# Weight sums, short convolution, input split and order of products in an FFN beside a long convolution

## The chip, the cores and the metric

The kernel runs on one core of a Trainium2 chip. Its time is the device time of one execution in microseconds (us). Three executions of the kernel before took 1178.04, 1177.70 and 1166.35 us, a median of 1177.7. The engines are named as in the profile: PE (TensorE's matmuls), PEld (its weight loads), DVE (VectorE), ACT (ScalarE), POOL (GpSimd), SP (SyncE, which here only issues transfers).

## The reference

Two branches read the normalized input and are added to it. All is float32, S = 2048 tokens, D = 576 channels, 4608 hidden units.

```python
x = A_q
xn = _layernorm(x)
# A: short causal convolution of k (4 taps), times v, long causal convolution by FFT, times xn
k_shift = sum over t of k_pad[:, t:t + S, :] * shift_k[:, 3 - t]
kv = k_shift * v
y = irfft(rfft(kv, 2 * S) * rfft(ssm_k, 2 * S))[:S] + kv * ssm_D
# B: FFN
h = maximum(xn @ w1, 0)
out = x + xn * y + h @ w2
```

## The kernel before

**FFN.** Tokens lie in 16 tiles t of 128; a tile is two half-tiles u of 64 rows. Four blocks b of 512 tokens are worked in two halves: blocks 0 and 1, then 2 and 3. Within a half, 18 steps g each take 256 hidden units, so there are 36 steps, called quads; g = 0 is done by plain products (classical), 1 to 35 by quad (L497). Every float32 factor is split in a high part of 12 bits and a rest, and a product of two is made of three matmuls (product, L455: two chunks of three, 128x512). One quad multiplies 2 x 2 blocks (two token blocks, two groups of 128 hidden units, with w1's rows in halves) by Winograd's scheme with seven products, named "00", "01", "s2", "s3", "11", "s1", "s4" after the operand of x, and adds the last 64 of the 576 rows by rest (L463, two matmuls). The scheme needs four sums of weights (sums, L407, on POOL: four adds of 128x256) and their splits wb and wc; wa, wd, wr and w2 are split from the weights as loaded (split_w, L399: a copy on ACT, a subtraction on POOL). Two banks of PSUM hold the products. Between products ACT copies a bank: y gets -x (L514, L538), u2 and p5 are kept in SBUF (L531, L558); DVE adds them in the bank (L559, L570); hidden (L467) applies Relu on ACT to hh and takes the rest ll on DVE.

Between the products stand eight units: unit(n) calls mm2 (L594), 12 matmuls of 128x288 for one tile of the quad before, summed in one of two buffers pso. The result is added to acc by DVE (L614). In units 1 and 5 of a quad (SEEDED) ACT instead copies acc into pso before the matmuls (L592) and out again (L611). The order of all FFN matmuls is fixed (done["pe"] in matmuls, L446).

**Convolution.** The generator conv (L650) yields costs; tick (after each product, rest and unit) lets it run when enough FFN cost has passed (rate, W_FB to W_FO, PAUSE). Its five stages are

- fb: normalize tokens 1024 to 2047, transpose them by DRAM, write the seven operands for the second half to DRAM (later_operands);
- fk: transform ssm_k: load kt, split by stack (L630, half of the partitions on ACT, half on DVE), two matmuls, store zk;
- fx: for each of 16 tiles t the short convolution: tap (L723, DVE: multiply and add), gate (times v), split for both half-tiles by stack (two ACT copies and two DVE subtractions of 64x576), four transforms (first, L636), stores of zx;
- fm: for 36 chunks of 512 columns: second transform of k and x, product of the spectra, and the way back. Every second chunk is "stacked": its high and low parts are stacked in the partitions by four transfers of POOL (turn, L846), so that the way back is two matmuls (back_stacked, L863) instead of three (back); its low sums go to zl;
- fo: for 32 half-tiles: load z, add zl to it by an accumulating transfer of POOL (add_z, L926), split (L946, L947), two matmuls (L994, L995), add of y, gate with x, add to acc or to the finished first half.

The scheduler of the language orders the instructions of an engine by its own clock; here() and at_turn(g) only keep side work behind the last acc or Relu. Weights are loaded from POOL's queue, everything else mostly from SP's queue, which issues in order and waits in order.

The last unit's results leave by SP and ACT.

## Time and profile before

| | |
|---|---|
| three executions | 1178.04, 1177.70, 1166.35 us |
| the profiled execution | 1173.84 us, of it 1171.8 between the first and the last instruction (the span) |
| mean granted clock of TensorE | 0.969 |
| matmuls | 6028, PE busy 1062.8 us |
| data moved by DMA | 194.94 MB |

Every row of times below is from that one execution. A group row gives the line of the kernel, the engine, the operation, what it writes and reads with sizes, how often, the busy time and the mean in ns. A row of waits gives the engine that stood, for whom, how long in total, how many times and the longest time. A row of a single line gives least, median and greatest duration in ns, and its first and last start. In the timeline the first two numbers are start and length in us. A busy PE isn't one at its peak, since ends of matmuls are modelled; the distance between two starts is exact. In the rows, psf is the PSUM of the convolution, psh the banks of the quads, pso the sums of the units, r a loaded weight, ohi and olo the high part and the rest of z.

### The profile page before, as it was taken

Reading aid. Unit: us, or ns where it says so; the run is one execution under the profiler, and the core shown is the slowest. Engines: PE = TensorE matmul, PEld = TensorE weight load, DVE = VectorE, ACT = ScalarE, POOL = GpSimd, SP = SyncE. Lnnn points to the kernel's source line nnn. Section 1 sums busy time; section 2 is a strip of 40 time slices with the busy share of each in tenths; the row PEclk is TensorE's granted clock in tenths of the full one; section 3 lists DMA queues with packets and bytes.
Section 4 is the critical chain, followed back from the end, with each engine's and each line's share of the span. In section 5 each row is a group of like instructions: output and inputs, shape, how many; then the busy total and the mean of one; then the engine's idle time right before and its main releaser. Section 6 shows DMA issues by size and latency. Waiting matters only on the chain. (4 is left out here: it accounts for less than half of the span.)

```text
span 1171.8 us, 17791 instructions
## 1 busy us (share of the span) xinstructions
PE 1062.8 (91%) x6028; PEld 932.2 (80%) x6028; DVE 839.0 (72%) x1154; ACT 730.9 (62%) x1358; POOL 629.6 (54%) x741
## 2 busy tenths in 40 slices
PE   7879899899997888899889999999999999789988
PEld 3758799789886777788789887888888887577977
DVE  5765653577666999988753777777777763889885
ACT  4524453688883455555444888889888974545751
POOL 4345465655544555656454555546566655565850
PEclk8989999899999999999889999999999999889999
DMA  6266459644448445448752566766677647865844
GB/s 166 59 156 156 155 194 179 110 144 150 143 147 209 129 149 168 152 131 297 259 162 83 167 184 170 197 167 182 198 201 199 188 130 214 197 178 134 237 111 102
DMA packets 139062, 194.94 MB, mean 166 GB/s; under 512 B 69757, under 2 KB 72447, under 8 KB 137180
## 3 DMA queue, kind: packets, MB, share of 16 engines
q1 hardware_dynamic: 111932, 126.71, 38.6%
q0 software_dynamic: 26720, 66.21, 22.0%
q10 hardware_dynamic: 320, 0.88, 0.3%
q8 instruction: 48, 0.79, 0.3%
q14 instruction: 42, 0.34, 0.1%
HBM read 129.27 MB, written 50.33 MB: 153 GB/s over the span
## 5 line engine op out<-in xcount | busy, mean ns | idle before, releaser
L451 PE MATMUL pso<-w,hh 128*128 128x288 f32 x2304 | 482.0, 299 | 18.4 <-DVE acc L614 18.4
L451 PEld LDWEIGHTS pso<-w,hh 128*128 128x128 f32 x2304 | 390.6, 191 | 49.0 <-DVE acc L614 27.8
L451 PE MATMUL pso<-w,ll 128*128 128x288 f32 x1152 | 343.3, 298 | 0.0
L614 DVE TENSOR_TENSOR acc<-pso,acc 128x576 f32<-128x576 f32 x220 | 165.6, 753 | 91.9 <-PE pso L451 90.3
L451 PEld LDWEIGHTS pso<-w,ll 128*128 128x128 f32 x1152 | 220.0, 191 | 1.5
L471 ACT ACTIVATE hh<-psh 128x512 fp32r<-128x512 f32 x140 | 83.4, 596 | 118.9 <-PE psh L451 64.7
L403 POOL TENSOR_TENSOR wc<-sums,wc 128x512 fp32r<-128x512 f32 x35 | 47.8, 1366 | 156.0 <-ACT wc L402 156.0
L451 PE MATMUL psh<-xs,wb 128*128 128x512 f32 x420 | 116.1, 408 | 14.6 <-ACT u L531 14.4
L403 POOL TENSOR_TENSOR w<-r,w 128x576 fp32r<-128x576 f32 x72 | 109.9, 1527 | 16.4 <-ACT w L402 16.4
L472 DVE SCALAR_TENSOR_TENSOR ll<-psh,hh 128x512 fp32r<-128x512 f32 x140 | 95.8, 684 | 31.3 <-ACT hh L471 30.8
L451 PE MATMUL psh<-x,wa 128*128 128x512 f32 x420 | 110.6, 399 | 6.6 <-ACT psh L514 3.2
L451 PEld LDWEIGHTS psh<-xs,wb 128*128 128x128 f32 x420 | 77.5, 194 | 32.0 <-ACT u L531 19.2
L451 PEld LDWEIGHTS psh<-x,wa 128*128 128x128 f32 x420 | 76.4, 190 | 23.5 <-ACT psh L514 5.9
L414 POOL TENSOR_TENSOR sums<-r 128x256 f32<-128x256 f32 x70 | 57.8, 861 | 60.8 <-DMA r<-in_w 55.7
L451 PE MATMUL psh<-hl,wr 128*128 128x512 f32 x280 | 89.6, 398 | 0.7 <-ACT p L558 0.7
L611 ACT ACTIVATE acc<-pso 128x576 f32<-128x576 f32 x68 | 44.1, 648 | 54.5 <-PE pso L451 53.8
L634 DVE TENSOR_TENSOR ks<-kt,ks 64x288 fp32r<-64x288 f32 x64 | 56.2, 878 | 26.5 <-ACT ks L633 25.2
L414 POOL TENSOR_TENSOR sums<-sums,r 128x256 f32<-128x256 f32 x70 | 69.1, 987 | 0.8
L403 POOL TENSOR_TENSOR wa<-r,wa 128x512 fp32r<-128x512 f32 x36 | 51.6, 1432 | 31.6 <-ACT wa L402 31.5
L846 POOL DMA_DIRECT2D st<-yl x72 | 36.0, 514 | 59.9 <-issue 49.2
L451 PE MATMUL psh<-x,wc 128*128 128x512 f32 x210 | 57.3, 409 | 7.9 <-ACT psh L538 7.9
L451 PE MATMUL psh<-xs,wc 128*128 128x512 f32 x210 | 56.1, 402 | 7.8 <-DVE ll L472 7.7
(163 smaller groups left out, 2133.1 us busy)
## 6 DMA issues: line engine op xcount, KB each, us to landing
r<-in_w POOLq DMA_DIRECT2D x70, 288.0 KB, 4.6
r<-in_w POOLq DMA_DIRECT2D x35, 512.0 KB, 4.9
zk<-zk SPq DMA_DIRECT2D x32, 288.0 KB, 2.5
zx<-zx SPq DMA_DIRECT2D x32, 288.0 KB, 2.9
ztk<-zk SPq DMA_DIRECT2D x36, 256.0 KB, 3.0
ztx<-zx SPq DMA_DIRECT2D x36, 256.0 KB, 3.2
k<-k SPq DMA_DIRECT2D x72, 128.0 KB, 2.9
zo<-zy SPq DMA_DIRECT2D x32, 288.0 KB, 4.6
```

What stands on the lines that cost most here:

```text
L403: nc.gpsimd.tensor_tensor(w[:, 1, :n], src, w[:, 0, :n], OP.subtract)
L414: nc.gpsimd.tensor_tensor(t[:, to], a, b, OP.add)
L451: last = nc.tensor.matmul(ps, a, m, start=start and n == 0, stop=n == len(seq) - 1, skip_group_check=True)
L471: done["act"] = nc.scalar.activation(hh, ps, AF.Relu)
L472: nc.vector.scalar_tensor_tensor(ll, ps, 0.0, hh, op0=OP.max, op1=OP.subtract)
L611: done["act"] = nc.scalar.activation(two(acc[t]), ps[:, :, :NH], AF.Copy)
L614: done["acc"] = nc.vector.tensor_tensor(two(acc[t]), ps[:, :, :NH], two(acc[t]), OP.add)
L634: nc.vector.tensor_tensor(dst[other], src[own], dst[own], OP.subtract)
L846: nc.gpsimd.dma_start(st[q * A2:(q + 1) * A2, i % GR, :], yl[i * A2:(i + 1) * A2, :])
```

## The change

- The sums of weights go from POOL to DVE, behind the last add of acc. In the second half (g > 18) wb and wc are not made again: the first half stores them to DRAM (parts_n), the second half loads them.
- The products of a quad stand in the order "00", "01", "s2", "s1", "s3", "s4", "11". What u2 and p5 are added to is written to SBUF, and Relu reads it there. Splits for the next quad are placed anew, and units 4, 5 and 6 follow one another. Units work block 0 before block 1; the first quad has its four units at the beginning.
- Which units are seeded by ACT depends on the stage: six of eight in fb and fx, none in fk and fm, four in fo.
- fx: only the first tap is written by DVE; the other three products are added to it by accumulating transfers from POOL. The sum is split in one ACT copy and one DVE subtraction of 128x576, stored to DRAM and loaded back as the two stacks. Each half of zx is stored by itself.
- fm: all chunks use three matmuls on the way back; turn, back_stacked and zl are gone. More buffers for loads.
- fo: add_z is gone.
- later_operands loads rows earlier and works in smaller pieces; the planner's weights, pauses and warm-up counts are set anew; in the start the splits of the first weights stand earlier, and sums(1) later.

The diff, cut to its core (of quad only the new text stands here; removed functions are in the kernel above):

```diff
-W_FK, W_FX, W_FM, W_FO = 1.4, 4.2, 2.24, 2.4
+W_FK, W_FX, W_FM, W_FO = 2.4, 2.9, 3.5, 2.6
-PAUSES = 19
-SHARE = 0.985
+PAUSES = 18
+SHARE = 0.975
-N_FB, W_FB = 32, 2.0
+N_FB, W_FB = 36, 2.5
-WARM_TILE = (0, 10, 0, 4)
+WARM_TILE = (0, 6, 0, 0)
...
         t = sums_w[g] = wp.tile([P, 4, 2, P], F32, tag="sums", name=f"sums{g}")
         w00, w01 = r1[:, 0:2, :P], r1[:, 0:2, P:]
         w10, w11 = r1[:, 2:4, :P], r1[:, 2:4, P:]
-        for to, a, b in ((3, w00, w01), (0, t[:, 3], w11), (2, t[:, 0], w10), (1, w11, w01)):
-            nc.gpsimd.tensor_tensor(t[:, to], a, b, OP.add)
+        with at_sums(g):
+            for to, a, b in ((3, w00, w01), (0, t[:, 3], w11), (2, t[:, 0], w10), (1, w11, w01)):
+                nc.vector.tensor_tensor(t[:, to], a, b, OP.add)
+
+    def at_sums(g):
+
+        return tc.issue_after(done["acc"].ins) if g > 1 else nullcontext()
 
     def split_a(g):
         wa[g] = split_w(g, "wa", raw1[g][:, 0:4, :P], (4, P))
 
+    def kept(g):
+        return g > NQ
+
+    def split_sums(g, kind, pair):
+
+        if kept(g):
+            w = wp.tile([P, 2, 4, P], F32R, tag=kind, name=f"{kind}{g}")
+            nc.sync.dma_start(w.bitcast(F32), parts_n[kind][g % NQ])
+        else:
+            w = split_w(g, kind, sums_w[g][:, pair].rearrange("p s c f -> p (s c) f"), (4, P))
+            if g < NQ:
+                nc.sync.dma_start(parts_n[kind][g], w.bitcast(F32))
+        return w
+
     def split_b(g):
-        src = (sums_w[g][:, 0:2].rearrange("p s c f -> p (s c) f") if g else
-               raw1[g][:, 0:2, P:])
-        wb[g] = split_w(g, "wb", src, (4, P))
+        if g:
+            wb[g] = split_sums(g, "wb", slice(0, 2))
+        else:
+            wb[g] = split_w(g, "wb", raw1[g][:, 0:2, P:], (4, P))
 
     def split_c(g):
-        wc[g] = split_w(g, "wc", sums_w[g][:, 2:4].rearrange("p s c f -> p (s c) f"), (4, P))
+        wc[g] = split_sums(g, "wc", slice(2, 4))
 
     def split_d(g):
...
     def hidden(g, b, f, ps):
-        k = dict(bufs=2 if b else 4)
-        hh = hp.tile([P, 512], F32R, tag=f"hh{b}", name=f"hh{g}_{b}_{f}", **k)
-        ll = hp.tile([P, 512], F32R, tag=f"ll{b}", name=f"ll{g}_{b}_{f}", **k)
+        k = dict(bufs=2 - (b or f))
+        hh = hp.tile([P, 512], F32R, tag=f"hh{b}{f}", name=f"hh{g}_{b}_{f}", **k)
+        ll = hp.tile([P, 512], F32R, tag=f"ll{b}{f}", name=f"ll{g}_{b}_{f}", **k)
...
         b0, b1 = (0, 1) if g < NQ else (2, 3)
         more = g + 1 < QUADS
+        x = bank(g, 0, "1")
+        y = bank(g, 1, "2")
         if units and units[0] is not None:
             open_unit(*units[0], 0)
+        product(x, wa[g], 0, "00", start=True)
+        nc.scalar.activation(y, x, AF.Copy, scale=-1.0)
+        later("00")
+        unit(0)
         split_w2(g, 0)
         if more:
             load_w2(g + 1, 0)
+        product(x, wa[g], 2, "01")
+        rest(x, g, b0, 0)
+        hidden(g, 0, 0, x)
+        later("01")
         unit(1)
+        product(y, wb[g], 0, "s2")
         u2 = hp.tile([P, 512], F32, tag="u2", name=f"u2_{g}", bufs=1)
+        nc.scalar.activation(u2, y, AF.Copy)
+        later("s2")
+        x = bank(g, 0, "5")
+        product(x, wc[g], 2, "s1", start=True)
+        p5 = hp.tile([P, 512], F32, tag="p5", name=f"p5_{g}", bufs=1)
+        nc.scalar.activation(p5, x, AF.Copy)
+        later("s1")
+        unit(2)
         split_w2(g, 1)
         if more:
             load_w2(g + 1, 1)
+            if not kept(g + 1):
+                sums(g + 1)
+        product(y, wb[g], 2, "s3")
+        later("s3")
+        unit(3)
+        if more:
+            split_a(g + 1)
+        rest(x, g, b0, 1)
+        later(2)
+        product(x, wd[g], 0, "s4")
+        later("s4")
+        nc.vector.tensor_tensor(u2, x, u2, OP.add)
+        x = bank(g, 0, "4")
+        nc.scalar.activation(x, y, AF.Copy, scale=-1.0)
+        hidden(g, 0, 1, u2)
+        unit(4)
+        if more:
             split_b(g + 1)
         unit(5)
         if more:
             split_d(g + 1)
+        unit(6)
+        rest(y, g, b1, 1)
+        nc.vector.tensor_tensor(p5, y, p5, OP.add)
+        product(x, wc[g], 0, "11")
+        later("11")
+        unit(7)
+        hidden(g, 1, 1, p5)
+        rest(x, g, b1, 0)
+        later(3)
+        hidden(g, 1, 0, x)
+        if more:
             split_r(g + 1)
+            split_c(g + 1)
             if g + 2 < QUADS:
                 load_w1(g + 2)
...
+    stage = {"seeded": ()}
 
     def open_unit(g, b, i, n):
 
         t = token(g, b, i)
         ps = open_ps[g, t] = ps_o.tile([P, 2, 512], F32, tag="o", name=f"pso{g}_{t}")
-        if n in SEEDED and 0 < g < QUADS - 1:
+        if n in stage["seeded"] and 0 < g < QUADS - 1:
             seeded.add(t)
             nc.scalar.activation(ps[:, :, :NH], two(acc[t]), AF.Copy)
...
+    def stacks(pool, src, t):
+
+
+        both = pool.tile([P, 2, D], F32R, tag="both", name=f"both{t}", bufs=1)
+        with here():
+            nc.scalar.activation(both[:, 0], src, AF.Copy)
+            nc.vector.tensor_tensor(both[:, 1], src, both[:, 0], OP.subtract)
+        nc.sync.dma_start(xs_n[t % 2].rearrange("u p k d -> (u p) k d"), both.bitcast(F32))
+        out = []
+        for u in range(U):
+            stk = pool.tile([P, D], F32R, tag="stk", name=f"xs{t}_{u}", bufs=3)
+            for k in range(2):
+                nc.sync.dma_start(stk[halves(k)[0]].bitcast(F32), xs_n[t % 2][u, :, k])
+            out.append(stk)
+        return out
...
+            stage["seeded"] = (0, 1, 3, 4, 5, 7)
             yield from later_operands(fp)
...
                     else:
-                        e = fp.tile([P, D], F32, tag="e", name=f"e{t}_{n}", bufs=1)
+                        e = fp.tile([P, D], F32, tag="e", name=f"e{t}_{n}", bufs=3)
                         nc.vector.tensor_tensor(e, win[t - n], sk[:, n, :], OP.mult)
-                        nc.vector.tensor_tensor(sums[t], sums[t], e, OP.add)
+                        nc.gpsimd.dma_start(sums[t], e, accum_op=OP.add)
...
-            def split(t, u):
+            def split(t):
                 if t < T:
-                    stks[t, u] = fp.tile([P, D], F32R, tag="stk", name=f"xs{t}_{u}", bufs=4)
-                    with here():
-                        stack(stks[t, u], sums[t], u)
+                    stks[t, 0], stks[t, 1] = stacks(fp, sums[t], t)
...
-            gate(0)
-            for u in range(U):
-                split(0, u)
-            yield -PAUSE / 8
             for n in range(KS):
                 tap(1, n)
                 yield -PAUSE / 8
+            gate(0)
+            split(0)
+            yield -PAUSE
             for t in range(T):
                 if t + 2 < T:
                     load(t + 2)
 
-                side = (((gate, t + 1),), ((split, t + 1, 0),),
-                        ((split, t + 1, 1),), ((tap, t + 2, 0),),
-                        ((tap, t + 2, 1),), (),
-                        ((tap, t + 2, 2),), ((tap, t + 2, 3),))
+                side = (((tap, t + 2, 0),), ((tap, t + 2, 1),),
+                        ((gate, t + 1),), ((split, t + 1),),
+                        ((tap, t + 2, 2),), ((tap, t + 2, 3),), (), ())
                 for u in range(U):
-                    z = fp.tile([P, D], F32, tag="z", name=f"zx_{t}_{u}")
                     for h in range(2):
                         cols = slice(h * NH, (h + 1) * NH)
-                        first(mats[t], stks[t, u][:, cols], z[:, cols], u)
+                        z = fp.tile([P, NH], F32, tag="z", name=f"zx_{t}_{u}_{h}", bufs=3)
+                        first(mats[t], stks[t, u][:, cols], z, u)
+                        nc.sync.dma_start(at_t(zx, T * u + t)[:, :, cols], z)
                         for part in range(2):
                             for what, *args in side[4 * u + 2 * h + part]:
                                 what(*args)
                             yield W_FX / 2
-                    nc.sync.dma_start(at_t(zx, T * u + t), z)
...
             def parted(n):
...
-                if stacked(n):
-                    yh = fp.tile([P, GR, CW], F32R, tag="st", name=f"st{n}")
-                    for r in range(GR):
-                        nc.scalar.activation(yh[:, r, :], y, AF.Copy)
-                    nc.vector.tensor_tensor(yl, y, yh[:, 0, :], OP.subtract)
-                else:
-                    yh = fp.tile([P, CW], F32R, tag="yh", name=f"yh{n}")
-                    nc.scalar.activation(yh, y, AF.Copy)
-                    nc.vector.tensor_tensor(yl, y, yh, OP.subtract)
+                yh = fp.tile([P, CW], F32R, tag="yh", name=f"yh{n}")
+                nc.scalar.activation(yh, y, AF.Copy)
+                nc.vector.tensor_tensor(yl, y, yh, OP.subtract)
...
-    quad(1, [None, None, *((0, 1, i) for i in range(BT))])
+    quad(1, [*((0, 1, i) for i in range(BT))])
     for g in range(2, QUADS):
-        quad(g, [(g - 1, b, i) for b in (1, 0) for i in range(BT)])
-    for b in (1, 0):
+        quad(g, [(g - 1, b, i) for b in range(2) for i in range(BT)])
+    for b in range(2):
```

More of the change, by code (lines that the diff above doesn't have):

```diff
@@ new lines, in later_operands @@
+        load_rows(first)
+        load_rows(first + 2)
+        yield -PAUSE
+        for t in range(first, T, 2):
+            pair = rows[t]
+            for i in range(2):
+                with here():
+                    stats(t + i, pair[:, i, :])
+                yield W_FB / 2
+            with here():
+                inv_std(t, 2)
+            for i in range(2):
+                with here():
+                    normalized(pair[:, i, :], pair[:, i, :], t + i)
+                yield W_FB / 2
+            nc.sync.dma_start(rows_n[t // BT - HB, t % BT // 2].rearrange("t p d -> p t d"), pair)
+            load_rows(t + 4)
@@ new lines, in later_operands, with load @@
+        yf, ws = {}, {}
+        order = [(b, c) for b in range(HB) for c in range(5)]
+        for b in range(HB):
+            for k in range(2):
+                yf[f"{b}{k}"] = pool.tile([P, 2, 512], F32, tag=f"xf{b}{k}", name=f"yf{b}{k}")
+        def load(n):
+            if n < len(order):
+                b, c = order[n]
+                src = rows_n[b].rearrange("h t (g p) d -> p (h t g) d", p=32)
+                w = ws[n] = pool.tile([P, 512], F32, tag="xw", name=f"xw{b}_{c}", bufs=4)
@@ L548, in quad @@
-        if last:
-            load_operand("11")
-        unit(4)
-        rest(c, g, b1, 1)
-        if last:
-            load_rest_operand(3)
-        unit(5)
-        e = bank(g, 0, "5")
-        product(e, wc[g], 2, "s1", start=True)
-        p5 = hp.tile([P, 512], F32, tag="p5", name=f"p5_{g}", bufs=1)
-        nc.scalar.activation(p5, e, AF.Copy)
-        nc.vector.tensor_tensor(c, c, p5, OP.add)
-        hidden(g, 1, 1, c)
-        if more:
-            split_c(g + 1)
-        if last:
-            load_operand("s1")
@@ L565, in quad @@
-        unit(6)
-        rest(e, g, b0, 1)
-        if last:
-            load_rest_operand(2)
-        product(e, wd[g], 0, "s4")
-        nc.vector.tensor_tensor(e, e, u2, OP.add)
-        hidden(g, 0, 1, e)
+            if not kept(g + 1):
[10 more added lines that the diff above has]
+        nc.vector.tensor_tensor(u2, x, u2, OP.add)
@@ L893, in conv @@
                     load(zx, n + 2, "x")
-                if 0 < n <= NCH and stacked(n - 1):
-                    turn(n - 1)
                 if n < NCH:
@@ L969, in add @@
                         added.add(t)
-            for n in range(5):
+            for n in range(6):
                 load_z(n)
```

243 lines of the change are left out of this document (90 added, 153 removed).

## The prediction

> **What bounds the kernel now.** I read the busy times first, then a table of stages (windows), then who waited for whom on PE, then single rows.
>
> ```profile
> PE 1062.8 (91%) x6028; PEld 932.2 (80%) x6028; DVE 839.0 (72%) x1154; ACT 730.9 (62%) x1358; POOL 629.6 (54%) x741
> ```
> ```profile
> 0.00:82.00 82.00, 60.55 (x281) 44.41 (x282) 53.83 (x128) 34.23 (x61) 30.98 (x40) 0.90 0.52 131
> 82.00:216.00 134.00, 128.47 (x754) 114.87 (x752) 70.07 (x99) 63.17 (x110) 77.97 (x87) 0.99 0.76 164
> 216.00:385.00 169.00, 152.26 (x903) 137.78 (x904) 117.02 (x146) 124.50 (x232) 88.09 (x104) 0.97 0.51 149
> 385.00:612.00 227.00, 202.30 (x1160) 180.17 (x1160) 197.77 (x232) 116.25 (x229) 123.67 (x130) 0.95 0.60 185
> 612.00:975.00 363.00, 351.55 (x1963) 305.98 (x1962) 249.01 (x352) 294.74 (x537) 200.92 (x249) 1.00 0.61 170
> 975.00:1040.00 65.00, 48.62 (x247) 41.01 (x246) 47.63 (x63) 31.95 (x64) 41.17 (x51) 0.87 0.86 219
> 1040.00:1172.00 132.00, 119.08 (x729) 107.96 (x727) 103.72 (x138) 66.05 (x128) 66.84 (x82) 0.98 0.57 145
> ```
> The columns are the stretch, its length, busy PE, PEld, DVE, ACT, POOL, granted clock, DMA share, GB/s. The stretches are: start; later operands (fb) with the load of ssm_k; fk; fx; fm; the beginning of fo; the rest. PE is the bound, but unevenly. Span less busy PE is 21.5, 5.5, 16.7, 24.7, 11.5, 16.4 and 12.9 us, 109 in all. In fx DVE is busy 198 of 227 us, in fm ACT 295 of 363.
>
> ```profile
> PE psf L994 <- DVE y L997: 19.0, 10, 4.5
> PE pso L451 <- DVE acc L614: 18.4, 17, 3.8
> PE psh L451 <- ACT u L531: 14.4, 10, 3.0
> PE psh L451 <- DVE ll L472: 10.8, 4, 7.4
> PE psh L451 <- ACT psh L538: 7.9, 10, 2.8
> PE psf L640 <- DVE xs L634: 4.1, 4, 2.0
> PE psh L451 <- ACT psh L514: 3.2, 5, 1.5
> PE psf L640 <- ACT wb L402: 3.2, 1, 3.2
> ```
> These eight rows make 81.0 us. They are what a change of order and of engines can win; the matmuls themselves stay.
>
> Two unit costs of PE come from start times in the timeline:
>
> ```profile
> 532.55 1.55 PE L451 MATMUL psh<-x,wa 128*128 128x512 f32 x6
> 533.94 0.62 PE L451 MATMUL psh<-hl,wr 128*128 128x512 f32 x2
> 534.40 0.42 PE L451 MATMUL pso<-w,hh 128*128 128x288 f32 x2
> ...
> 535.98 0.39 PE L451 MATMUL psh<-xs,wb 128*128 128x512 f32 x1
> ```
> A product (6 matmuls) takes 533.94 - 532.55 = 1.39 us, 0.23 each; a rest 0.46; a unit (12 matmuls, from 534.40) 1.58. A quad of 50 + 8 units is 50 x 0.23 + 8 x 1.58 = 24.2 us.
>
> **The change part by part.**
>
> *Order of products (A).* The copy of u2 had to finish behind one unit (1.58 us); now product "s1" and unit(2) cover it, 2.97 us. The negated copy for "11" had unit(3), 1.58; now it has units 4, 5, 6 and a rest, 5.2 us. The combinations c+p5 and e+u2 go to SBUF, so Relu and ll no longer hold a bank. The new product "s1" needs the bank of hidden(0,0), which has unit(1) and product "s2", 2.97 us, for a Relu and an ll. Of 14.4 + 7.9 + 3.2 = 25.5 us I take off 17 (the first copy, L514, keeps its cover), of 10.8 for ll I take 7, since the 7.4 us one is a queue on DVE behind late rows and the first quad now does four units before it needs those banks. A = -24; bounds 0 and -36.
>
> *Weight sums to DVE, half of them kept (B).* They leave POOL, and so do half of wb and wc.
>
> ```profile
> L414 POOL TENSOR_TENSOR sums<-r x70: 717/736/1302, 20.5 to 1108.1; 128x256 f32<-128x256 f32 x70
> L414 POOL TENSOR_TENSOR sums<-sums,r x70: 721/859/2569, 23.0 to 1125.8; 128x256 f32<-128x256 f32 x70
> L403 POOL TENSOR_TENSOR wc<-sums,wc x35: 1270/1292/2002, 32.6 to 1128.9; 128x512 fp32r<-128x512 f32 x35
> L947 DVE TENSOR_TENSOR olo<-zo,ohi x32: 737/759/5390, 989.6 to 1135.2; 128x576 fp32r<-128x576 f32 x32
> L734 DVE TENSOR_TENSOR c<-c,e x48: 742/758/1864, 368.7 to 593.4; 128x576 f32<-128x576 f32 x48
> L634 DVE TENSOR_TENSOR xs<-c,xs x32: 751/755/2414, 380.5 to 599.7; 64x576 fp32r<-64x576 f32 x32
> L614 DVE TENSOR_TENSOR acc<-pso,acc x220: 737/757/759, 34.2 to 1166.6; 128x576 f32<-128x576 f32 x110
> ```
> (ns: least/median/most.) DVE gains 4 x 18 = 72 adds of 128x256. No row shows one; between nothing and the 0.76 of 128x576 I take 0.45, 32 us. It loses 48 adds of c (0.76 each, 36 us) and 32 half-width xs for 16 full ones (12 us): about -16 net. More comes from a second effect. acc, which reads PSUM and SBUF, never takes over 759 ns; olo, with two SBUF inputs, takes up to 5390. The timeline shows why:
>
> ```profile
> 998.69 1.71 POOL L414 TENSOR_TENSOR sums<-r 128x256 f32<-128x256 f32 x2
> 999.02 3.21 DVE L947 TENSOR_TENSOR olo<-zo,ohi 128x576 fp32r<-128x576 f32 x1
> 1000.06 1.55 POOL L403 TENSOR_TENSOR wa<-r,wa 128x512 fp32r<-128x512 f32 x1
> ```
> olo ends only after both POOL groups have ended. The second half of the kernel loses 4 sums and 2 splits a quad from POOL, of eleven operations. The Trainium skill (SBUF — State Buffer, section "SBUF: two separate sides") says that the ports these two engines share are an exclusive lock held for a whole instruction, by a DVE operation with two SBUF inputs as well; the row agrees for POOL holding DVE. By that rule the 72 new adds would hold POOL's splits in turn, and with their 32 us charged in full the sum would be 1170; no row here shows that direction. With DVE lighter, I take off half of the 18.4 us for acc: B = -9, bounds 0 and -18. ACT loses 34 copies of wb and wc. In their place SP stores 34 parts of 512 KB in the first half and loads 34 in the second. The load of wc waits for the last product "11" of the quad before, and SP's z, k and v transfers stand behind it; PE needs wc after unit(7), a rest, "00", unit(0), "01", a rest, unit(1) and "s2": 9.8 us, and
>
> ```profile
> r<-in_w POOLq DMA_DIRECT2D x35, 512.0 KB, 4.9
> ```
> lands in 4.9 us. So it costs nothing; without that cover up to 4.9 x 17 = 83 us. The wr split is now issued last in a quad and needed after 1.39 + 1.58 + 1.39 = 4.4 us: also covered unless POOL stands.
>
> *fo without the second part of z (C).* Its 32 accumulating transfers go, and POOL's sums with them, the ones that held olo at 999. PE's 19.0 us for y are waits for DVE behind such rows: C = -14, bounds 0 and -19.
>
> *fm (E).* Each of 18 stacked chunks goes from 2 matmuls to 3: 18 x 0.23 = +4. 72 POOL transfers, 18 copies to st and 18 of vo go, and so do the seeds of fm; PE's idle time there is only 11.5 us, so I count no gain beyond A.
>
> *fx by DMA (D).* This is the dearest unknown.
>
> ```profile
> k<-in_k SPq DMA_DIRECT2D x32, 144.0 KB, 4.1
> zx<-zx SPq DMA_DIRECT2D x32, 288.0 KB, 2.9
> wx<-in_fwd POOLq DMA_DIRECT2D x16, 256.0 KB, 4.1
> rows_n<-xn SPq DMA_DIRECT2D x4, 576.0 KB, 4.2
> zo<-zl POOLq DMA_DIRECT2D x32, 144.0 KB, 4.6
> ```
> ```profile
> 474.25 1.16 SPq L173 DMA_DIRECT2D k<-in_k  x2
> ```
> ```profile
> 550.00:600.00 50.00, 44.59 (x249) 39.79 (x250) 40.94 (x48) 23.71 (x47) 23.28 (x26) 0.93 0.79 260
> ```
> For each of 16 t three adds of 288 KB run on POOL's queue, each behind the landing of the one before: at 4.6 us as for zo, a chain of 14 us, in which weight splits and loads of POOL's queue stand. Then both (576 KB) is stored, and four loads of 144 KB wait for it, about 8.3 us by rows_n and k. SP issues 13 transfers a t (4 zx, 2 k, 2 v, 1, 4), at 0.58 us 7.5 us. Bytes: 1408 KB a t before (k, v, zx, wx), and 864 + 576 + 576 more, 3424 KB. By the planner's weights (64 x 2.9 at 1583 units of FFN cost, 53,248 a quad) fx is meant to last 5.5 quads, 5.5 x 24.2 + 128 x 0.13 = 150 us, 9.4 a t. With the quads' own weights (2240 KB each with the stores) that is 56.1 + 12.6 = 68.7 MB, 458 GB/s. At 260/0.79 = 329 GB/s, the rate of the busiest stretch at a full share, it takes 209 us, +59; at the 260 that a stretch really showed, 264 us, +114. The lower end is 0: a transform goes into PE's order where it is ready in the planner's clock, so a late one moves behind later quads; before, 64 x 4.2 x 1888 units were 9.5 quads, and the 227 us of fx held (1160 - 128) / 146 = 7, since it began late and still ended in step. I take +8, near the lower end by that row. The Trainium skill (DMA: Bandwidth & Descriptors, "Specifications") puts the ceiling at 435 GB/s; by it the 68.7 MB would take 158 us, D would be +8 and the sum the same; no run here shows that rate.
>
> *Units back to back (F).* Units 4, 5 and 6 now follow each other with no product between them. Unit 6 needs the bank of unit 4, so the add of acc (0.76) has 1.58 us, 0.82 of it for what stands ahead on DVE. Bounds: 0, and 2.0 us in each of 35 quads, 70, if two such operations of 0.76 and the POOL split of 1.29 that holds one stand ahead. I take +5, since acc itself never stretches and in fb and fx ACT does three quarters of the units.
>
> *Clock (G).* 1 - clock times length is 8 (start), 5 (fk), 11 (fx), 8 us (fo's beginning); much of it lies in the waits themselves. With a third of the waits gone I take -6, bounds 0 and -12.
>
> *Rest.* Eight warm-up matmuls fewer and the split of the start: 0, they lie in waits for rows.
>
> Sum: -24 - 9 - 14 + 8 + 4 + 5 - 6 = -36. The profiled execution is 1173.8 us (span 1171.8), 0.3% under the median of 1177.7: **1138 us**.
>
> **The rivals.** (1) *fx is bound by its transfers.* The order on PE is fixed, PE stands at the transforms. For it: 458 GB/s asked, 329 shown; the chain of 14 us against 9.4 a t. Against it: fx slid in the kernel before. Price 87, the middle of 59 and 114, for the 8 taken: 1138 + 79 = 1217, slower. It decides as soon as fx costs 51 us more than I take: then 1% over the median, 1189, is passed. (2) *Units 4 to 6 wait for DVE* in each quad, 70 for 5: 1203. For it: DVE at 198/227 in fx and two-input adds that stretch; against it: POOL is lighter. (3) *The waits only change their names*: the copies were waited for because ACT and DVE were full, not because of the order; A and B fall away: 1138 + 33 = 1171, within 1%. (4) *All eight rows go*: 1173.8 - 81 + 4 = 1097.
>
> **How the numbers follow.** Chances: the forecast 0.60, (1) 0.14, (2) 0.08, (3) 0.10, (4) 0.08. What a measurement of this kernel can tell from no change is about 1%, 1166 to 1189. Faster is the forecast and (4), 0.68; same is (3), 0.10; slower (1) and (2), 0.22. The range leaves out most of (1), which lies above it, and half of (4), together under 0.2: 1100 to 1205. The forecast alone spans 1110 to 1165.
>
> **What would show it.** Right: the rows for u, for the negated copy and for y fall below 5 us each; olo stays near 0.76; fm near 97% PE. Wrong on D: PE rows "psf from a DMA" or "from both" in fx over 30 us, DMA share near 1 there. Wrong on F: PE waiting for acc by more than 18 us. Wrong on B: DVE's sums or POOL's splits at the top of PE's waits.

## The result, and the profile after

The changed kernel takes 1216.0 us (median; 1211.2 to 1221.4) where the kernel before took 1177.9 beside it: a ratio of 1.034, interval 1.025 to 1.043. It is slower, 78 us above the forecast and within 1 us of rival (1). The profiled execution took 1218.6 us, its span 1216.8.

The busy times, and the stages as stretches (columns as before): rest of fk and beginning of fx, fx, fm, 40 us at the beginning of fo, the rest.

```profile
PE 1077.7 (89%) x6038; PEld 951.2 (78%) x6038; DVE 756.6 (62%) x1163; ACT 693.9 (57%) x1299; POOL 451.6 (37%) x511
```
```profile
400.00:439.00 39.00, 28.71 (x150) 24.62 (x149) 22.28 (x30) 16.14 (x31) 18.98 (x20) 0.91 0.95 239
439.00:727.00 288.00, 243.64 (x1370) 219.18 (x1369) 138.35 (x188) 123.28 (x248) 131.01 (x147) 0.92 0.98 284
727.00:1040.00 313.00, 302.68 (x1673) 264.99 (x1672) 226.47 (x339) 232.01 (x419) 87.46 (x94) 0.99 0.64 189
1040.00:1080.00 40.00, 19.66 (x63) 14.41 (x64) 21.36 (x36) 17.80 (x34) 6.10 (x10) 0.63 0.81 235
1080.00:1217.00 137.00, 120.88 (x744) 110.59 (x743) 93.31 (x144) 76.31 (x146) 40.51 (x53) 0.95 0.54 157
```
DVE, ACT and POOL all became lighter, and still PE stands longer. fx took 288 us with the DMA engines busy 0.98 of it (227 us at 0.60 before). At the beginning of fo PE works less than half of 40 us. The waits of PE, and what ACT's copy of zx waits for:

```profile
PE psh L479 <- ACT psh L545: 22.0, 13, 3.8
PE psf L682 <- DMA xs<-xs_n: 21.2, 7, 8.0
PE pso L479 <- ACT acc L637: 12.5, 10, 3.5
PE psf L997 <- DVE y L1000: 11.1, 10, 3.0
PE psf L997 <- ACT ohi L952: 7.4, 1, 7.4
PE psh L479 <- DMA wc<-wc_n: 6.7, 1, 6.7
...
PE psh L479 <- ACT psh L582: 2.2, 1, 2.2
PE psh L479 <- ACT u L558: 0.5, 1, 0.5
```
```profile
ACT zx L683 <- DMA zx<-zx: 47.2, 14, 7.9
```
The rows for u and for the later negated copy (now L582) did fall, from 14.4 and 7.9 to 0.5 and 2.2. In their place the first negated copy (L545) rose from 3.2 to 22.0. ACT's copies of zx stood 47.2 us until the stores of zx left their buffers. The rows for y and ohi all lie in those 40 us of fo, less 1.7. The row for wc, 6.7 us once, is a load of a kept part, which was to cost nothing.

### The profile page after: what moved, and what is told of

The parts are those of the page before. It is cut to its first block, busy times and chain, and to the rows that moved or that the text cites. A ratio compares the mean times of both kernels' runs of the same rounds, so it can differ in the third digit from the quotient of the medians.

```text
span 1216.8 us, 17720 instructions
## 1 busy us (share of the span) xinstructions
PE 1077.7 (89%) x6038; PEld 951.2 (78%) x6038; DVE 756.6 (62%) x1163; ACT 693.9 (57%) x1299; POOL 451.6 (37%) x511
## 3 DMA queue, kind: packets, MB, share of 16 engines
q0 software_dynamic: 27616, 70.86, 22.9%
## 5 line engine op out<-in xcount | busy, mean ns | idle before, releaser
L479 PE MATMUL pso<-w,hh 128*128 128x288 f32 x2304 | 488.5, 302 | 17.7 <-ACT acc L637 12.5
L640 DVE TENSOR_TENSOR acc<-pso,acc 128x576 f32<-128x576 f32 x210 | 157.8, 753 | 152.9 <-PE pso L479 138.7
L479 PE MATMUL psh<-x,wa 128*128 128x512 f32 x420 | 117.4, 414 | 27.5 <-ACT psh L545 22.0
L411 POOL TENSOR_TENSOR wr<-r,wr 128x256 fp32r<-128x256 f32 x36 | 34.6, 962 | 171.4 <-ACT wr L410 164.6
L479 PEld LDWEIGHTS psh<-xs,wb 128*128 128x128 f32 x420 | 75.6, 189 | 12.5 <-ACT u L558 0.8
L618 ACT ACTIVATE pso<-acc 128x576 f32<-128x576 f32 x78 | 51.0, 654 | 45.9 <-DVE acc L640 44.8
L411 POOL TENSOR_TENSOR wd<-r,wd 128x256 fp32r<-128x256 f32 x36 | 32.1, 893 | 120.9 <-ACT wd L410 120.7
L683 ACT ACTIVATE zx<-psf 128x288 f32<-128x288 f32 x64 | 25.2, 410 | 89.5 <-DMA zx<-zx 47.2
L779 POOL DMA_DIRECT2D c<-e x48 | 43.7, 917 | 64.4 <-issue 18.3
L500 DVE SCALAR_TENSOR_TENSOR ll<-psh,hh 128x512 fp32r<-128x512 f32 x70 | 47.9, 684 | 25.1 <-ACT hh L499 25.0
L479 PEld LDWEIGHTS psh<-xs,wc 128*128 128x128 f32 x210 | 39.3, 192 | 24.7 <-DVE ll L500 9.9
```

Source lines behind the costliest of these rows:

```text
L411: nc.gpsimd.tensor_tensor(w[:, 1, :n], src, w[:, 0, :n], OP.subtract)
L479: last = nc.tensor.matmul(ps, a, m, start=start and n == 0, stop=n == len(seq) - 1, skip_group_check=True)
L500: nc.vector.scalar_tensor_tensor(ll, ps, 0.0, hh, op0=OP.max, op1=OP.subtract)
L618: nc.scalar.activation(ps[:, :, :NH], two(acc[t]), AF.Copy)
L640: done["acc"] = nc.vector.tensor_tensor(two(acc[t]), ps[:, :, :NH], two(acc[t]), OP.add)
L683: nc.scalar.activation(z, ps[:, :NH], AF.Copy)
```

## The experiments

Each run's median stands beside its ratio to the kernel before, which ran beside it (medians 1171 to 1178 us). Differences between runs are of medians; where the ratios give another size, it stands beside.

### The input's way, part by part

**taps_dve** takes the adds back to DVE:

```diff
-                        nc.gpsimd.dma_start(sums[t], e, accum_op=OP.add)
+                        nc.vector.tensor_tensor(sums[t], sums[t], e, OP.add)
```


> After, with the three adds of each short convolution back on DVE (the split still goes by way of DRAM). In the changed kernel DMA is busy 0.97 of 400 to 730 us, 320 us of all 16 engines, and the 48 accumulating transfers are 6144 packets of 2304 B at 195 ns, about 75 us of that. Transfers bound fx by their sheer volume: demand falls to 245 us, fx is no longer full, PE's idle time there falls from 55 to about 25 us, 1185 us. The chain of three adds in a row is what is late, not the volume: the chain is gone here too, so the same 1185 us; this run alone does not tell the two apart. The planner's shorter fx is the cause: PE still stands as before, 1210 us or more.

Measured: 1158.2 us, 0.989 (0.984 to 0.994).

**split_direct** splits straight into the stacks, as the kernel before:

```diff
-                    stks[t, 0], stks[t, 1] = stacks(fp, sums[t], t)
+                    for u in range(U):
+                        stks[t, u] = fp.tile([P, D], F32R, tag="stk", name=f"xs{t}_{u}", bufs=4)
+                        with here():
+                            stack(stks[t, u], sums[t], u)
```


> After, with the input split by ACT and DVE straight into the stacked operand (no store to DRAM and no loads from it; the adds still go by DMA). Volume: the bounce is 18.9 MB, 8192 packets of 2304 B at 93 ns, 48 us of all 16 engines out of 320; fx is relieved by up to that, 1190 us, DMA share near 0.85 to 0.9. Chain: only the landing of a store and a load behind the adds goes, the adds stay: 1205 us, and PE now waits for the xs split, with POOL's DMA behind it. Planner: 1210 us or more.

Measured: 1172.1 us, 1.004 (0.999 to 1.008).

**both_undone** has both edits.

> After, with both parts of the input's way by DMA undone: adds on DVE, split direct. Volume or chain: DMA share in fx near 0.65, PE's idle time in fx near the 25 us of the kernel before, 1165 to 1175 us, a little under the kernel before since fk's 10 us and fm's 4 us of gain remain. Planner (fx put into too few quads, or the new order of products costs time): 1195 us or more, although the transfers are gone.

Measured: 1159.1 us, 0.991 (0.987 to 0.995). All three runs came out below every time that was expected of them. So D (the input's way by DMA; the stores of zx by halves stay in all these runs) cost 57 us by the medians, 51 by the ratios. The parts do not add up: the way by DRAM alone costs -1 us (taps_dve), the adds by DMA alone 13 (split_direct), the two together 57.

**ballast** is both_undone with a load that nobody needs, 48 adds by DMA into unused tiles (and one buffer of the stacks fewer, 3 for 4):

```diff
+                        nc.gpsimd.dma_start(junk[n % 2], e, accum_op=OP.add)
```


> As the kernel with both parts undone, but each tap's product is also added by DMA into one of two unused tiles, so the 48 accumulating transfers of 288 KB are there as a load and nothing waits for their result except the buffers of the products. Volume: as the kernel with only the direct split, within 10 us (about 1190), since the same bytes move at the same cost. Chain: as the kernel with both undone, within 10 us (about 1170), since no work waits for the sums.

Measured: 1164.2 us, 0.996 (0.992 to 1.000). This is within 10 us of both_undone, as the chain of transfers would have it, but also within 10 us of split_direct, as volume would: it does not decide, since one part of the load alone is cheap, as with taps_dve. **full_volume** has the load of both parts and waits for one: taps_dve with two plain stores of e for each add.

```diff
+                        for i in range(2):
+                            nc.gpsimd.dma_start(junk[n - 1, i], e)
```


> The kernel with the adds back on DVE (1158 us), the split still by way of DRAM, and each tap's product stored twice to unused places in DRAM: two plain transfers of 288 KB stand for one accumulating transfer, whose packets took about twice as long (195 against 93 ns). So fx moves as much DMA time as the changed kernel, but no sum waits for a transfer. If fx is bound by volume, the two parts of the input's way cost 57 us only together because together they pass what the DMA engines can do: 1195 to 1220 us here too, DMA share 0.97 over the same 300 us. If it is the chain (three adds in a row, then store, then load, each behind the landing of the one before), 1158 to 1172 us, with a DMA share as high but PE not waiting.

Measured: 1201.7 us, 1.024 (1.020 to 1.027). No sum waits for those stores, only the buffers of e (1.8 us in all), and they cost 43 us over taps_dve (41 by the ratios). So most of D is volume. The chain is left with 14 us (1216.0 - 1201.7), or 8 between split_direct and ballast, which move the same adds with and without a chain; the intervals touch in both pairs. The stretch of fx in the five, in the order taps_dve, split_direct, both_undone, ballast, full_volume:

```profile
431.00:645.00 214.00, 189.54 (x1087) 168.53 (x1086) 153.84 (x200) 112.01 (x227) 96.22 (x92) 0.96 0.97 306
```
```profile
431.00:669.00 238.00, 210.07 (x1183) 188.14 (x1182) 147.77 (x188) 129.82 (x253) 125.14 (x143) 0.93 0.93 260
```
```profile
427.00:613.00 186.00, 161.79 (x905) 143.36 (x904) 161.17 (x207) 116.20 (x230) 74.32 (x77) 0.94 0.73 229
```
```profile
417.00:643.00 226.00, 189.91 (x1056) 168.42 (x1057) 183.41 (x225) 122.41 (x244) 115.49 (x133) 0.92 0.98 266
```
```profile
435.00:717.00 282.00, 253.39 (x1501) 229.51 (x1502) 187.26 (x239) 131.09 (x263) 153.47 (x203) 0.96 0.98 344
```
Length times DMA share is the time that all 16 engines worked: 136 us without the two parts, 208 with the way by DRAM, 221 with the adds (ballast and split_direct alike), 276 in full_volume, 282 in the changed kernel. Except in both_undone these are nearly the lengths of fx themselves: with either part fx lasts as long as its transfers, and yet that costs little. What costs may then be how much later it ends, which the next three runs try.

### Where the lateness is paid

**old_weights** gives the changed kernel the plan of the kernel before:

```diff
-W_FK, W_FX, W_FM, W_FO = 2.4, 2.9, 3.5, 2.6
+W_FK, W_FX, W_FM, W_FO = 1.4, 4.2, 2.24, 2.4
```


> The changed kernel with the stages' weights of the kernel before (1.4, 4.2, 2.24, 2.4 for fk, fx, fm, fo), nothing else: fx is planned over 9.2 quads and not 5.5, with the same transfers and the same chain. If the length that the plan gives fx decides, both volume and chain fit in 9.2 quads (223 us): 1160 to 1180 us, and the transforms of fo no longer stand in a row at its beginning. If the transfers cost what they cost wherever they stand, 1205 us or more.

Measured: 1221.7 us, 1.041 (1.037 to 1.044). The plan's length of fx does not decide. fx began later and ended where it had ended, with the DMA engines full (the share of 1.04 shows that this column can be some per cent too high); the beginning of fo is the same:

```profile
465.00:730.00 265.00, 231.55 (x1321) 207.19 (x1322) 126.14 (x165) 137.28 (x273) 125.88 (x143) 0.95 1.04 304
730.00:1040.00 310.00, 300.55 (x1662) 263.58 (x1662) 226.88 (x337) 230.85 (x416) 86.91 (x92) 0.99 0.64 191
1040.00:1080.00 40.00, 19.65 (x62) 13.90 (x62) 21.24 (x36) 18.91 (x36) 7.07 (x11) 0.64 0.76 233
```

**late_fo** plans fo later in the changed kernel:

```diff
-W_FK, W_FX, W_FM, W_FO = 2.4, 2.9, 3.5, 2.6
+W_FK, W_FX, W_FM, W_FO = 2.4, 2.9, 3.87, 1.97
```


> The changed kernel (1216 us) with two weights of the plan changed, 3.87 for fm and 1.97 for fo (3.5 and 2.6 before): the sum of the plan stays, so fk and fx stay where they are, and fo is planned 1.2 quads later. In the changed kernel fx ends on PE 3.7 quads later than in the kernel without the transfers (22.3 against 18.6), and fo's first transforms, which were planned before fm had ended, run in a row from 1051 to 1078 us with PE idle half of the time (33 us lost there against 3). If that row of transforms is a cost of its own, caused by the lateness and paid at fm's end, it shrinks: 1185 to 1195 us. If fx's lateness has to be paid somewhere in any case, 1210 us or more, with the idle time at another place, such as the end of fo.

Measured: 1208.8 us, 1.031 (1.027 to 1.036), between the two expected: 7 us less, inside the interval of the changed kernel, and not 25 or more. In its profiled execution (1202.7 us, the fastest of the four) the transforms of fo no longer stand in a row, but PE's row for y is still 14.7 us, and from 1040 us to the end PE stands 29 us, where in the changed kernel it stands 36. The plan of fo is not the whole of the loss.

**late_fx** makes fx late in both_undone without any transfer more, and plans fm shorter, so that fo stays where it was:

```diff
-PAUSES = 18
+PAUSES = 30.3
-W_FK, W_FX, W_FM, W_FO = 2.4, 2.9, 3.5, 2.6
+W_FK, W_FX, W_FM, W_FO = 2.4, 2.9, 2.35, 2.6
-            yield -1.5 * PAUSE
+            yield -13.8 * PAUSE
```


> The kernel with both parts of the input's way undone (1159 us), but fx delayed in the plan by 3.7 quads (197,000 units of the plan's clock) and fm planned that much shorter (weight 2.35 for 3.5), so fo is planned where it was. Nothing more is moved than there; only fx is as late on PE as in the changed kernel (its last transform after 22.3 quads). If the lateness is what costs, paid in a row of fo's transforms at fm's end: 1185 to 1200 us, with PE waiting for y and for ohi as in the changed kernel. If the transfers themselves cost it, 1157 to 1168 us.

Measured: 1175.8 us, 1.002 (0.999 to 1.006), 17 us over both_undone (14 by the ratios), again between the two expected: lateness, without the transfers, costs 17 of the 57. From 400 us on, its stretches (before fx, fx, fm, the beginning of fo), and then both_undone's (its fx stands above):

```profile
400.00:508.00 108.00, 100.89 (x588) 90.36 (x588) 40.97 (x67) 61.48 (x111) 45.56 (x49) 0.98 0.44 131
508.00:690.00 182.00, 160.18 (x886) 142.40 (x887) 144.02 (x186) 116.35 (x229) 65.54 (x73) 0.93 0.78 243
690.00:1000.00 310.00, 308.01 (x1737) 273.44 (x1736) 241.65 (x343) 234.94 (x419) 90.99 (x95) 1.00 0.66 194
1000.00:1040.00 40.00, 19.09 (x65) 13.75 (x65) 21.80 (x37) 19.19 (x36) 7.09 (x12) 0.66 0.79 234
```
```profile
400.00:427.00 27.00, 16.22 (x82) 13.88 (x81) 17.21 (x24) 10.31 (x19) 6.18 (x7) 0.87 0.73 199
...
613.00:967.00 354.00, 345.47 (x1947) 306.45 (x1946) 257.07 (x371) 242.58 (x432) 105.23 (x115) 1.00 0.61 185
967.00:1007.00 40.00, 38.48 (x231) 34.67 (x230) 22.35 (x35) 23.44 (x45) 15.06 (x18) 1.00 0.81 252
```
```profile
PE 1059.1 (91%) x6038; PEld 938.0 (81%) x6038; DVE 818.9 (71%) x1227; ACT 708.4 (61%) x1315; POOL 417.6 (36%) x463
```
The beginning of fo is that of the changed kernel: 19.1 us of PE in 40, a clock of 0.66, where both_undone has 38.5 and 1.00. The waits there, in the changed kernel and in late_fx, are the same to 0.2 us:

```profile
PE psf L997 <- DVE y L1000: 9.4, 9, 3.0
PE psf L997 <- ACT ohi L952: 7.4, 1, 7.4
PE psf L849 <- ACT yh L871: 3.4, 1, 3.4
```
```profile
PE psf L1000 <- DVE y L1003: 9.5, 9, 2.4
PE psf L1000 <- ACT ohi L955: 7.2, 1, 7.2
PE psf L852 <- ACT yh L874: 3.4, 1, 3.4
```
So this part is shown to come from the lateness, with the fm that it shortens, and not from the transfers. full_volume has it too, at the end of an fx that was as late:

```profile
1022.00:1062.00 40.00, 21.00 (x65) 14.94 (x66) 21.43 (x36) 17.72 (x34) 5.22 (x8) 0.59 0.77 219
```
Such 40 us hold some 65 matmul records, against 231 in both_undone: transforms of fo in a row, each waiting for the one before to be emptied by ACT and DVE, with few FFN matmuls between.

### The order of products

**old_order** is both_undone with the quad, the order of units and the hidden buffers of the kernel before (and its smaller numbers of buffers in fb, fx and fo, since one more pair of hidden buffers has to fit; the choice of seeded units by stage stays); **fewer_buffers** is the new order with those numbers.

```diff
-        k = dict(bufs=2 - (b or f))
+        k = dict(bufs=2 if b else 4)
...
-        quad(g, [(g - 1, b, i) for b in range(2) for i in range(BT)])
+        quad(g, [(g - 1, b, i) for b in (1, 0) for i in range(BT)])
```


> The kernel with both parts of the input's way undone (1159 us), with the order of products, of units and of the hidden buffers of the kernel before (one more pair of hidden buffers, so fewer buffers in fb, fx and fo, as many as the kernel before had there). The new order was forecast to bring 24 us: then 1180 us or more. If the waits only changed their names (the row for the first negated copy grew from 3 to 18 us while those for u and the other negated copy fell by 20), 1155 to 1165 us.

> The kernel with both parts undone (1159 us), new order, with the smaller numbers of buffers that the run with the old order had (3 for 4 of xw in fb, 1 for 3 of e in fx, 5 for 6 of zo and 2 for 3 of xt in fo). If the 8 us between the two orders come from the order, this stays at 1157 to 1163 us; if they come from the buffers (later loads, so less that stands ahead in the queues), it falls to 1152 or below.

Measured: 1150.8 us, 0.981 (0.977 to 0.984), for the old order; 1163.5 us, 0.989 (0.980 to 0.997), for the new one with fewer buffers. The buffers are not the reason; the new order, with its places for units and splits, costs 8 to 13 us. Of the rows, u rises to 7.1 in the old order, but PE's wait for ACT's copy of acc, the end of a seeded unit, falls from 16.3 to 5.2. The first negated copy waits as long in both (18.2 in both_undone; 21.0 in the old order, 10.2 of it once).

**early_hidden** tries the cause of the row L545. In both_undone:

```profile
437.14 1.75 DVE L500 SCALAR_TENSOR_TENSOR ll<-p,hh 128x512 fp32r<-128x512 f32 x1
...
440.69 0.68 DVE L500 SCALAR_TENSOR_TENSOR ll<-psh,hh 128x512 fp32r<-128x512 f32 x1
...
441.40 0.58 ACT L545 ACTIVATE psh<-psh 128x512 f32<-128x512 f32 x1 [2.29 <-DVE ll L500]
...
442.04 1.42 PE L479 MATMUL psh<-x,wa 128*128 128x512 f32 x3 [2.89 <-ACT psh L545]
```
The copy writes the bank that hidden(1,0), the last step of the quad, has just read; DVE's ll ends at 441.37, and the copy starts.

```diff
-        unit(7)
-        hidden(g, 1, 1, p5)
         rest(x, g, b1, 0)
         later(3)
         hidden(g, 1, 0, x)
+        unit(7)
+        hidden(g, 1, 1, p5)
...
-        k = dict(bufs=2 - (b or f))
+        k = dict(bufs=1 + (f == 0))
```


> The kernel with both parts undone (1159 us), new order kept, but the last part of a quad changed: the last rest and hidden(1,0) come before unit(7), and hidden(1,0) gets a second pair of buffers (paid for by fewer buffers in fb, fx and fo, as in the run with the old order). The trace shows the next quad's first negated copy waiting for the ll of hidden(1,0), which reads the bank that the copy writes. If that is what the row of 18 us for the copy is, it falls below 8 us and the time to 1145 to 1152 us; if ACT and DVE are simply late there, the row stays, or another grows, and the time stays at 1159 us, within 5.

Measured: 1149.6 us, 0.978 (0.974 to 0.983). The row fell to 10.6, not below 8, and the row for ll rose from 13.6 to 30.6; the time fell by 10 us all the same (14 against fewer_buffers). So it pays to work hidden(1,0) earlier; that it pays through this row is not shown, since the row for ll rose by more than this one fell.

### The weight sums

From both_undone, **not_kept** neither stores nor loads parts of the weights (the diff), and **sums_pool** moreover puts the sums back on POOL (nc.gpsimd for nc.vector in sums).

```diff
-        return g > NQ
+        return False
...
-            if g < NQ:
-                nc.sync.dma_start(parts_n[kind][g], w.bitcast(F32))
```


> The kernel with both parts of the input's way undone (1159 us), and the sums of the weights back on POOL in all quads, no parts stored or loaded: the change to the sums is undone. It was forecast to bring 9 us: 1168 us or more, with olo stretched to several us behind POOL's sums and PE waiting for y and acc. If the sums on DVE brought nothing, 1155 to 1162 us.

> The kernel with both parts undone (1159 us), sums on DVE in all quads, no parts stored or loaded. The stores and loads were forecast to cost nothing, and to spare ACT 34 copies, POOL 34 splits and DVE 68 adds in the second half. If so, 1163 to 1170 us. In the trace ACT's copy of wc waited 6.7 us for the store of the wc before it, at 221 us, and PE lost 4.5 us to it; 34 MB less is moved in all. If keeping costs more than it spares, 1150 to 1156 us.

Measured: 1163.1 us, 0.993 (0.990 to 0.997), for sums_pool and 1152.2 us, 0.985 (0.980 to 0.990), for not_kept. (One of not_kept's four executions took 2928 us, and nothing here tells why; the figures are of the other three, 1151.7 to 1156.6.) The sums on DVE bring 9 us by the ratios, 11 by the medians. Keeping takes about 7 of it back, though its interval overlaps that of both_undone. The one place in both_undone where ACT waits for a store of wc:

```profile
215.15 2.09 SPq L443 DMA_DIRECT2D wc_n<-wc  x1
...
221.04 0.63 ACT L410 ACTIVATE wc<-sums 128x512 fp32r<-128x512 f32 x1 [6.75 <-DMA wc_n<-wc]
...
221.57 0.58 ACT L545 ACTIVATE psh<-psh 128x512 f32<-128x512 f32 x1
...
222.20 1.22 PE L479 MATMUL psh<-x,wa 128*128 128x512 f32 x2 [4.48 <-ACT psh L545]
```
The copy of wc waits until the store of the last wc has left the one buffer, and the negated copy stands behind it on ACT.

**hidden_late_c** moves that copy, **hidden_not_kept** drops the stores, both in early_hidden:

```diff
         unit(0)
+        if g > 1:
+            split_c(g)
...
             split_r(g + 1)
-            split_c(g + 1)
```


> The kernel with the last rest and hidden(1,0) before unit(7) (1149.6 us), and the split of wc moved from the end of a quad to behind unit(0) of the next, so that ACT's wait for the store of wc stands behind the negated copy and no longer in front of it. If the row for the first negated copy (10.6 us there) is ACT waiting for wc's buffer, it falls below 6 us and the time to 1143 to 1147 us; if not, 1149 us, within 4, or worse where wc then comes late for its product.

> The kernel with the last rest and hidden(1,0) before unit(7) (1149.6 us), with no parts of the weights stored or loaded: sums and splits in all quads. Keeping cost 4.7 us with the order of the change (1159.1 against 1154.4). If the two are independent, 1143 to 1146 us; if the early hidden already took away the wait that the stores caused, 1149 to 1153 us.

Measured: 1145.9 us, 0.979 (0.974 to 0.985), and 1156.1 us, 0.981 (0.974 to 0.988). Neither differs from early_hidden beyond the intervals, so whether the two edits add anything stays open, and with it what keeping costs in that order; the row for the first negated copy stayed at 9.8 and 9.9. The gains do not simply add up. The fastest versions, about 2% under the kernel before (0.978 to 0.981), are early_hidden, hidden_late_c, old_order and hidden_not_kept.

## Why the prediction was wrong, point by point

Without the input's way the forecast was 1138 - 8 = 1130; both_undone measured 1159. With D at 57 for 8 both errors have the same sign: 29 + 49 = 78.

**D failed.** The step was "I take +8, near the lower end by that row": a late transform moves behind later quads, as before, and costs nothing. The bounds held. That rival (1)'s 1217 was met is luck: it put D at 87, where 57 was measured, and A and F at -19, where the new order cost 8 to 13. Its mechanism, PE standing at the transforms, is only a part of the loss (21.2 us in the row for xs). The transforms did move: counted in PE's order (146 FFN matmuls to a quad), the last transform of fx stands after 22.2 quads in the changed kernel and 18.4 in both_undone, in late_fx 21.7. But the room behind fx is limited. fm, 354 us in both_undone, is 313 in the changed kernel and 310 in late_fx, so it takes in some 40 us. An fx that is 28 us longer than that of both_undone (taps_dve) costs -1, 40 longer (ballast) 5, 52 (split_direct) 13, 96 (full_volume) 43, 102 (the changed kernel) 57.

Against both_undone the changed kernel's span is 57.4 us longer. By place, as span less busy PE: 20 more from 400 us to fx's end (10.3 + 44.4 against 10.8 + 24.2), 19 at fo's beginning (20.3 against 1.5), 2 in fm. PE's busy time is 18.6 longer for the same 6038 matmuls, at a mean granted clock of 0.942 against 0.965 (10.9 longer at 0.951 in late_fx, without the transfers): time lost to waits is partly paid again in clock.

The working of D had sizes wrong, in both directions. I counted the adds like other bytes. Against both_undone (186 x 229 = 42.6 MB in 136 us of all engines, 3.2 us a MB) taps_dve moved 22.9 MB more in 72 us, 3.1 us a MB; ballast 17.5 MB more in 85 us. Of these 14.2 MB are the adds (48 x 0.295); with the other 3.3 at 3.2 us a MB, 75 us are left for them, 5.3 us a MB. The chain was longer than worked out, too: in the changed kernel an add landed in 8.0 us (4.6 taken), the store of both in 6.4 and a load of xs in 7.1 (8.3 taken for the two). On the other side 329 GB/s was no ceiling: full_volume moved 344 over all of its fx. The Trainium skill (DMA: Bandwidth & Descriptors, "Specifications") has the ceiling at 435 GB/s; no run here reached that, and the changed kernel, with its engines full, moved 284.

My sign for D, over 30 us of PE waiting for psf from a DMA, did not appear (21.2), though the other, a DMA share near 1, did. Where the scheduler moves late work, lateness is seen only in part as a wait at its own place.

**A and F failed together.** -24 + 5 was forecast; the new order costs 8 to 13. The rows for u and the negated copy fell as worked out, and I said the first copy "keeps its cover". It does not: in the new order hidden(1,0) is the last step of a quad and reads the bank which that copy writes. In part this is rival (3), names that change. F was sized for DVE's acc, and that row is 2.8 us in the changed kernel and 0.4 in both_undone and fewer_buffers; the wait came from ACT, which copies the seeded units out (12.5, 16.3 and 16.8). No run separates A from F. A also put u2 and p5 into SBUF at no cost. There ll reads both its inputs from SBUF, as olo does in the prediction's row, and it stretches, while ll from a bank does not. Before, and then both_undone:

```profile
L472 DVE SCALAR_TENSOR_TENSOR ll<-psh,hh x140: 637/684/694, 57.4 to 1153.6; 128x512 fp32r<-128x512 f32 x140
```
```profile
L500 DVE SCALAR_TENSOR_TENSOR ll<-psh,hh x70: 665/684/693, 57.3 to 1135.5; 128x512 fp32r<-128x512 f32 x70
...
L500 DVE SCALAR_TENSOR_TENSOR ll<-p,hh x35: 616/682/1908, 73.6 to 1134.9; 128x512 fp32r<-128x512 f32 x35
```
The ll of 1.75 us at 437.14, ahead of the late one in the timeline above, is of this kind: it runs beside POOL's split of wc. What this costs of the 8 to 13 us no run shows.

**B was right in a part, wrong in its sum.** -9 was forecast with nothing for keeping; the sums brought 9 to 11, and keeping took about 7 back, so that B as a whole brought 3 to 4 (sums_pool against both_undone, where the intervals overlap). I had covered the loads and not asked who waits for the stores. DVE's adds took 0.42 us (0.45 estimated). The rule of the Trainium skill on the shared ports (SBUF — State Buffer, "SBUF: two separate sides") would have them hold POOL's splits. The trace agrees where they meet, which is seldom: in the changed kernel 6 of the 72 adds overlap work of POOL, and the two splits of wa that began inside an add took 1422 and 1445 ns, for a median of 1296 over all 36 (1303 before). So the rule cost little here because the adds rarely met a split, not because it failed.

```profile
L423 DVE TENSOR_TENSOR sums<-r x36: 393/418/957, 27.8 to 556.0; 128x256 f32<-128x256 f32 x36
...
L953 DVE TENSOR_TENSOR olo<-zo,ohi x32: 737/758/2609, 1051.8 to 1200.5; 128x576 fp32r<-128x576 f32 x32
```
**C** was right by its rows where fo begins on time: the row for y is 0.5 us in both_undone (19.0 before), and olo at most 2865 ns there (5390 before; 2609 in the changed kernel); no run puts add_z back, so its -14 us are not measured by themselves. In the changed kernel the lateness gave 11.1 back. **E** showed its sign: fm is 97% PE (302.68 of 313). **G** had the wrong sign: the mean clock fell from 0.969 to 0.942. All terms but A, D and F come to -25 forecast and -22 measured (old_order against the kernel before beside it). That is luck in part: B brought less than its 9, and G's 6 did not come there either (clock 0.968).

What stays open: how much of the 17 us of late_fx, and of the 20 us inside fx, would be left with a plan made for them; which of the rows of early_hidden, where ll rose, is its bound; and how the cost of the new order divides among A, F and the ll that reads from SBUF.

## What to carry to other kernels

Work moved from engines to DMA has to be counted in engine time of the transfers against the time that the stage may take, adds by their own rate; two such moves that are each free may together pass the limit. Where a scheduler can push late work behind other work, ask how much room stands behind it and where it ends: part of the loss shows at the next border, not where the transfers are. When an operand moves from PSUM to SBUF, look for the other engine that the operation may then wait for. When an order of steps is changed, follow each bank and each single buffer once around the loop, over its end into the next turn.

## What the runs showed of the hardware

The accumulating transfers from POOL's queue needed about 1.7 times the DMA time of the other transfers of fx per byte (5.3 against 3.2 us a MB; packets of 2304 B in the fx of the changed kernel took a median of 195 ns accumulating and 107 ns plain). The DMA engines could be busy 0.97 of 214 us, at 306 GB/s, without loss to the kernel (taps_dve). In full_volume single slices reached 385 GB/s:

```profile
GB/s 162 82 200 215 206 212 175 125 134 177 194 162 173 255 315 349 334 336 385 361 367 349 346 249 237 184 190 192 186 185 200 184 208 140 209 172 170 174 146 143
```
The clock granted to PE fell to 0.63 in 40 us in which PE was half idle, and to 0.66 in late_fx; both_undone had 1.00 at the same DMA share (0.81 in both it and the changed kernel). So it went with PE's idleness, not with the transfers. A DVE operation with two SBUF inputs (ll from p5) took up to 1.91 us beside POOL's splits, where the same operation with one input in PSUM never passed 0.69 (both_undone).
